# Decayed block attention ahead of two expert layers: the attention's outputs in two PSUM banks, one for each head parity

## The chip, the cores and the metric

The kernel runs on one core of a Trainium2 chip. The metric is the device time of one execution in microseconds (us), the median of three. The engines are named as the profile names them: PE (TensorE, the matrix engine; its weight loads are listed as PEld), DVE (VectorE), ACT (ScalarE), POOL (GpSimd) and SP (SyncE, which issues most of the DMAs).

## The reference

Three stages follow each other, all in fp32. The first is attention with a decay for each of 8 heads (batch 2, 768 positions, head size 64), worked out block by block with a state that is carried on:

```python
for b in range(nb):
    intra = einsum('bhic,bhjc->bhij', qb, kb) * Dmask
    intra = einsum('bhij,bhjd->bhid', intra, vb)
    inter = einsum('bhid,bhde->bhie', qb * lam_pow, kv_state)
    out[:, :, sl] = intra + inter
    kv_state = lam_block * kv_state + einsum('bhsd,bhse->bhde', kb * rev_pow, vb)
```

Its output, 1536 tokens of 512 values, goes through a dense mixture of 4 experts (every token through every expert, 512 to 1024 to 512, weighted by given probabilities), and then through a second mixture of 8 experts in which each token goes to the one that its gate chooses.

## The kernel before

**Stages.** The attention works in 12 chunks, named c, of 128 positions of one batch; even and odd c are the two batches. Its steps are mixed into the first unit of the first expert layer (k = 0, groups of 256 tokens at t0 = 0, 256 and 512). The list `asteps` and the table `paces` fix which attention step stands after which matmul group. The whole program is inside `tc.manual_schedule()`: each engine runs its instructions in the order in which the code lists them, so an instruction that waits holds up everything behind it on its engine. After the attention come the units of the first layer (PE lines 462 and 586), the routing, and the second layer.

**One chunk.** The 8 heads are held as 4 pairs h with a member r (0 or 1): head = 2h + r. Queries and keys of member r stand in partitions 64r to 64r+63.

- `att_qk(c)` (line 357): 8 products of keys by queries into two PSUM tiles, one for each r. Each uses 64 rows of the array and all 128 columns.
- `att_a(c)` (line 392): DVE multiplies these by the decay mask, into `a`.
- `att_qd(c)` and `att_kd(c)` (lines 368, 375): POOL makes the decayed queries `qd` and keys `kd`.
- `att_o(c)`: for c of 2 and more, 8 products of queries by state (line 410), each of 64 rows by 64 columns of the array with 128 columns streamed; then 8 products of values by `a` (line 416), each of 128 rows by 64 columns, added on top in PSUM. The output of a head is 64 partitions by 128 columns of the tile `xo`, one PSUM bank; member r has partitions 64r and up. So at line 410 a head with r = 0 uses the upper left quarter of the array and a head with r = 1 the lower right one. The result is then moved out of PSUM. For the first 6 chunks that is `hi_lo`: ACT rounds it into `xh` (line 171) and DVE takes the rest into `xl` (line 172). For the last 6 it is one ACT copy into `x2` (line 422).
- `att_u(c)`, for c below 10: 8 products of `kd` by values (line 434), 128 rows by 64 columns, 64 columns streamed, into the PSUM tile `u`, which has a bank of its own; DVE adds them to the decayed state (line 447, or copies them for c below 2, line 440), and POOL decays the state before (line 443).

At the very end of the second layer the last output tile `zr`, one PSUM bank, is moved out by two engines: DVE scales columns 0 to 255 (line 1265) and ACT columns 256 to 511 (line 1269), into separate halves of the result.

PSUM has 8 banks: 3 for `ps_mm`, 3 for `ps_qk`, and one each for `xo` and `u`. The tile framework puts a semaphore wait wherever two engines touch the same tile and it sees a conflict.

Each fp32 product is two matmul instructions on PE, each with its weight load, so the 8 products of a line are 16 instructions in the trace.

Of the kernel before, what the change touches and what calls it, by code (L numbers as in the profile page):

```python
# [8 lines left out]
F32 = mybir.dt.float32  # L9
# [9 lines left out]
P = 128  # L19
B, H, S, D = 2, 8, 768, 64  # L20
CH = 128
NCH = S // CH
NC = B * NCH
HP = H // 2
N = B * S
DM = H * D
KD = DM // P
E1, FF = 4, 1024
# [36 lines left out]
def body(ctx: ExitStack, tc: tile.TileContext, lam, att, dp, w1a, w2a, wg, wgt, w1b, w2b, out):  # L65
    nc = tc.nc
    V, A, G, T, SP = nc.vector, nc.scalar, nc.gpsimd, nc.tensor, nc.sync

    def pool(name, bufs, **kw):
        return tc.tile_pool(name=name, bufs=bufs, **kw)  # L70
# [6 lines left out]
    ps_mm = ctx.enter_context(pool("ps_mm", 3, space=PSUM))  # L77
# [83 lines left out]
    st = {}  # L161
# [8 lines left out]
    def hi_lo(hi, lo, src, eng):  # L170
        A.copy(out=hi, in_=src)  # L171
        eng.tensor_tensor(out=lo, in0=src, in1=hi.bitcast(F32), op=ALU.subtract)  # L172
# [122 lines left out]
    xh = xp.tile([P, KD, TS], F32R, name="xh")  # L295
    xl = xp.tile([P, KD, TS], F32R, name="xl")
    x2 = xp.tile([P, KD, TS], F32, name="x2")
# [4 lines left out]
    ps_qk = at_ctx.enter_context(pool("ps_qk", 3, space=PSUM))  # L302
    ps_xo = at_ctx.enter_context(pool("ps_xo", 1, space=PSUM))
# [8 lines left out]
    def load_att(c, half):  # L312
        if c >= NC:
            return
        t = ab.tile([P, 2, 512], F32, tag=f"att{half}", name=f"att{half}_{c}")
        at_t[c, half] = t
        SP.dma_start(out=t, in_=att[c, :, 2 * half:2 * half + 2, :])
# [26 lines left out]
    aw = {}  # L344
# [50 lines left out]
    def att_o(c):  # L395
        t = at_t[c, 1]
        v = t[:, 1, :].rearrange("p (h r d) -> p h r d", h=HP, r=2)
        first = c < B
        a = aw.pop((c, "a"))
        pl, tag = (ps_mm, "mm") if c == 1 else (ps_xo, "xo")  # L400
        xo = pl.tile([P, HP, CH], F32, tag=tag, name=f"xo{c}")


        heads = [(h, r) for h in range(HP) for r in range(2)]
        if not first:
            qd = aw.pop((c, "qd"))
            st = st_t[c]
            for h, r in heads:
                q = slice(64 * r, 64 * r + 64)
                T.matmul(  # L410
                    xo[q, h, :], st[q, h, :], qd[q, h, :], start=h == 0, stop=False,
                    skip_group_check=True,
                )
        for h, r in heads:
            q = slice(64 * r, 64 * r + 64)
            T.matmul(  # L416
                xo[q, h, :], v[:, h, r, :], a[r][:, h, :], start=first, stop=True,
                skip_group_check=not first,
            )
        g, o = divmod(c * CH, TS)  # L420
        if g:
            A.copy(out=x2[:, :, o:o + CH], in_=xo)
        else:
            hi_lo(xh[:, :, o:o + CH], xl[:, :, o:o + CH], xo, V)

    def att_u(c):
        t = at_t.pop((c, 1))
        v = t[:, 1, :].rearrange("p (h r d) -> p h r d", h=HP, r=2)
        if c < NC - B:
            kd = aw.pop((c, "kd"))  # L430
            u = ps_xo.tile([P, HP, D], F32, tag="u", name=f"u{c}")
            for h in range(HP):
                for r in range(2):
                    T.matmul(
                        u[64 * r:64 * r + 64, h, :], kd[:, h, r, :], v[:, h, r, :],
                        start=True, stop=True,
                    )
            sn = ab.tile([P, HP, D], F32, tag="st", name=f"st{c}", bufs=3)
            if c < B:
                V.tensor_copy(out=sn, in_=u)  # L440
            else:
                sd = st_t.pop(c)
                G.tensor_tensor(
                    out=sd, in0=sd,
                    in1=rq[:, :, CH - 1:CH].to_broadcast([P, HP, D]), op=ALU.mult,
                )
                V.tensor_tensor(out=sn, in0=sd, in1=u, op=ALU.add)
            st_t[c + B] = sn
        load_att(c + 2, 1)
# [431 lines left out]
    with tc.manual_schedule():  # L881
# [15 lines left out]
            out=upper, in_=upper, compare_op=ALU.is_ge, fill=1.0, base=0,  # L897
# [20 lines left out]
        att_a(0)  # L918
        att_a(1)
        att_o(0)  # L920
        att_kd(0)
        load_piece()
        load_piece()
        att_qd(0)
        att_o(1)
        split_to(0, 0)
        att_qd(1)
# [285 lines left out]
        def moe2_mm1_rows(e, h, hook):  # L1213
            hi, lo, _ = xg[e]
            wh, wl = wt[0, K1 + 2 * e + h]
            n = CAPS[e]
            ps = ps_mm.tile([P, 512], F32, tag="mm", name=f"gr{e}_{h}")
            for d in range(KD):
                mm3(ps[:n], [((hi[:, d, :], lo[:, d, :]), (wh[:, d, :], wl[:, d, :]))],
                    d == 0, d == KD - 1)  # L1220
                if d < KD - 1:
                    hook(h * KD + d)
            g = gp.tile([P, HF], F32, tag="gr", name=f"gr{e}_{h}")
            A.activation(out=g[:n], in_=ps[:n], func=AF.Relu)
            hook(h * KD + KD - 1)
            return g
# [83 lines left out]
        for e in range(E2):  # L1310
# [28 lines left out]
            if CAPS[e] <= P:  # L1339
                for h in range(2):  # L1340
                    g = moe2_mm1_rows(e, h, hook1)
# [22 lines left out]
    with tc.If(n_r > 0):  # L1364
        with pool("op", 1) as op:
# [12 lines left out]
                out=upto, in0=tiles_e, scalar1=float(P), scalar2=None, op0=ALU.mult  # L1378
            )
            V.tensor_copy(out=base, in_=upto)  # L1380
            for e in range(1, E2):
                V.tensor_tensor(
                    out=upto[:, e:e + 1], in0=upto[:, e:e + 1], in1=upto[:, e - 1:e], op=ALU.add
# [4 lines left out]
                out=pick, in0=desc.unsqueeze(1).to_broadcast([P, NC, E2]),  # L1388
# [3 lines left out]
                out=own_t, in0=pick, in1=base.unsqueeze(1).to_broadcast([P, NC, E2]), op=ALU.mult  # L1392
# [4 lines left out]
                out=own_t, in0=pick,  # L1397
# [5 lines left out]
                out=pos_o, in0=few, scalar=float(FAR), in1=slot, op0=ALU.mult, op1=ALU.add  # L1403
            )
            V.tensor_tensor(
                out=own, in0=steps.unsqueeze(2).to_broadcast([P, OMAX, E2]),
# [7 lines left out]
                out=rest.rearrange("(n p) w -> p n w", p=P),  # L1414
                in_=none.unsqueeze(1).to_broadcast([P, OMAX, W]),
            )
            for t in range(NC):
                G.indirect_dma_start(
                    out=rest, out_offset=bass.IndirectOffsetOnAxis(ap=pos_o[:, t:t + 1], axis=0),
                    in_=acc[:, t, :], in_offset=None, bounds_check=OMAX * P - 1, oob_is_err=False,  # L1420
                )
            with tc.For_i(0, n_r, 1) as i:
# [8 lines left out]
                for w, src in enumerate((w1b, w2b)):  # L1431
                    for h in range(2):
                        SP.dma_start(
                            out=ws[w][h],
                            in_=src[bass.ds(e_r, 1), h].rearrange("e p f m -> p (e f) m"),
# [16 lines left out]
                for f in range(2 * FC):  # L1452
                    T.matmul(
                        ps, ht[:, f, :], ws[1][f // FC][:, f % FC, :], start=f == 0,
                        stop=f == 2 * FC - 1,
# [3 lines left out]
                    out=y, in0=ps, scalar1=xb[:, DM:DM + 1], scalar2=None, op0=ALU.mult  # L1459
                )  # L1460
                G.indirect_dma_start(
                    out=out,
                    out_offset=bass.IndirectOffsetOnAxis(ap=xb.bitcast(I32)[:, DM + 1:W], axis=0),
                    in_=y, in_offset=None, bounds_check=N - 1, oob_is_err=False,
# [3 lines left out]
def layouts(q, k, v, lam, moe_domain_probs, moe_w1, moe_w2, moe2_w_gate, moe2_w1, moe2_w2):  # L1468
    import numpy as np

    def tposed(a):
        a = a.reshape(B, HP, 2, NCH, CH, D)
        return a.transpose(3, 0, 2, 5, 1, 4).reshape(NC, P, HP * CH)

    def plain(a):
        a = a.reshape(B, H, NCH, CH, D)
        return a.transpose(2, 0, 3, 1, 4).reshape(NC, CH, DM)

    def back(a):
        return a.reshape(B, H, NCH, CH, D)[:, :, :, ::-1].reshape(B, H, S, D)  # L1480

    kr, vr = back(k), back(v)
    att = np.stack([tposed(q), tposed(kr), plain(kr), plain(vr)], axis=2)

    def first(w):
        return w.reshape(-1, KD, P, 2, HF).transpose(0, 3, 2, 1, 4)

    def second(w):
        return w.reshape(-1, 2, FC, P, DM).transpose(0, 1, 3, 2, 4)

    return {
        "lam": np.concatenate(
            [np.tile(lam.reshape(HP, 2).T.reshape(1, H), (P, 1)),
             np.repeat(lam.reshape(HP, 2).T, D, axis=0)], axis=1),
        "att": att,
        "dp": moe_domain_probs.reshape(B, NCH, P, E1).transpose(2, 1, 0, 3).reshape(P, NC, E1),
        "w1a": first(moe_w1),
        "w2a": second(moe_w2),
        "wg": moe2_w_gate.reshape(KD, P, E2).transpose(1, 0, 2),
        "wgt": moe2_w_gate.T,  # L1500
        "w1b": first(moe2_w1),
        "w2b": second(moe2_w2),
    }
# [18 lines left out]
```

## Time and profile before

| | us |
|---|---|
| median of 3 runs (761.99 to 762.12) | 762.01 |
| the profiled execution, its own time | 761.43 |
| its span, first to last instruction | 759.6 |
| PE busy | 744.5 |
| DVE busy | 491.6 |
| ACT busy | 307.6 |
| POOL busy | 92.6 |

The span is the time between the first and the last instruction; the execution's own time lies 1.8 us above it. An engine's busy time counts neither its waits nor its register and semaphore instructions.

### The profile page before, as it was taken

To read this page: it belongs to the slowest core of one execution; us is meant where nothing else is said; L and a number is where in the kernel's file an instruction comes from. 1 tells how busy PE (TensorE), PEld (TensorE's weight loads), DVE (VectorE), ACT (ScalarE), POOL (GpSimd) and SP (SyncE) were. 2 spreads that over 40 slices of the span, in tenths; PEclk is the share of its full clock that TensorE was granted. 3 is DMA by queue.
4 is the path that set the end of the run, shared out by engine and by line. 5 is a ranking of instruction groups with operands and counts; after the bars stand their busy time and mean duration, and the time that the engine had idled before them with its cause. 6 is when DMAs were issued, how large, how long until landed. Compare 5 with 4: busy or idle time off the path is not lost.

```text
span 759.6 us, 12447 instructions
## 1 busy us (share of the span) xinstructions
PE 744.5 (98%) x4736; PEld 671.7 (88%) x4736; DVE 491.6 (65%) x1073; ACT 307.6 (40%) x664; POOL 92.6 (12%) x98
## 2 busy tenths in 40 slices
PE   8999999999999999999999999999999999999995
PEld 7888889898898988889898898988998998998994
DVE  6443277766757668565377777768457877675883
ACT  3222335353442535245132141522124756665673
POOL 4554320000000000000000000002111013121013
PEclk9999999999999999999999999999999999999998
DMA  9765107436361113016261633287113867855660
GB/s 299 258 223 167 57 35 269 166 140 249 111 249 57 56 55 106 34 50 233 120 242 62 236 103 148 75 282 241 43 55 117 296 220 227 309 184 185 241 223 29
DMA packets 34313, 122.59 MB, mean 161 GB/s; under 512 B 4113, under 2 KB 6161, under 8 KB 31179
## 3 DMA queue, kind: packets, MB, share of 16 engines
q1 hardware_dynamic: 32139, 115.47, 44.0%
q0 software_dynamic: 2112, 6.31, 2.2%
q8 instruction: 38, 0.62, 0.3%
q14 instruction: 24, 0.20, 0.1%
HBM read 96.04 MB, written 25.92 MB: 161 GB/s over the span
## 4 chain that ended last, share of the span: by engine, by line
PE 87%; issue 4%; DVE 4%; DMA 2%; SPq 1%; ACT 1%; POOL 0%; POOLq 0%; ACTq 0%
PE y L462 35%; PE b L586 21%; PE h L462 9%; PE g L462 5%; PE z L462 3%; PE zr L1255 2%; PE qk L357 1%; PE z L1179 1%; PE xo L416 1%; PE xo L410 1%; DMA att<-in_att 1%; PE g L1179 1%; DVE w1l L172 1%; PE gr L462 1%; PE xt L1161 1%
## 5 line engine op out<-in xcount | busy, mean ns | idle before, releaser
L503 DVE SCALAR_TENSOR_TENSOR acc<-y,p_sb,acc 128x512 f32<-128x512 f32 x84 | 63.0, 750 | 65.4 <-PE y L462 62.2
L172 DVE TENSOR_TENSOR w1l<-raw,w1h 128x512 fp32r<-128x512 f32 x124 | 82.6, 689 | 16.8 <-ACT w1h L171 16.5
L171 ACT CAST w1h<-raw 128x512 fp32r<-128x512 f32 x128 | 75.4, 617 | 0.0
L593 ACT COPY u<-b 128x384 f32<-128x384 f32 x66 | 31.1, 474 | 100.3 <-PE b L586 98.9
L462 PE MATMUL h<-xh,w0h 128*128 128x256 f32 (+1 forms) x208 | 57.9, 308 | 1.2 <-ACT w0h L171 1.2
L462 PE MATMUL h<-xh,w0l 128*128 128x256 f32 (+1 forms) x208 | 56.2, 299 | 0.0
L172 DVE TENSOR_TENSOR w0l<-raw,w0h 128x512 fp32r<-128x512 f32 x80 | 51.6, 684 | 6.6 <-ACT w0h L171 6.0
L171 ACT CAST w0h<-raw 128x512 fp32r<-128x512 f32 x98 | 55.7, 619 | 0.2
L586 PE MATMUL b<-xh,w0h 128*128 128x384 f32 x176 | 48.9, 338 | 0.0
L641 POOL IOTA places<- 128x7 f32 x1 | 0.2, 160 | 385.9 <-PE y L462 385.9
L112 POOL DMA_INDIRECT out<-y,xb x16 | 29.3, 1832 | 135.8 <-DVE y L1295 84.9
L462 PEld LDWEIGHTS h<-xh,w0h 128*128 128x128 f32 x208 | 38.2, 188 | 2.8 <-ACT w0h L171 1.4
L462 PEld LDWEIGHTS h<-xh,w0l 128*128 128x128 f32 x208 | 38.4, 189 | 0.4
L462 PE MATMUL g<-xg,w0h 128*128 128x288 f32 (+1 forms) x192 | 38.1, 293 | 0.0
L600 DVE TENSOR_TENSOR u<-b,u 128x384 f32<-128x384 f32 x66 | 36.4, 551 | 2.4 <-PE b L586 2.4
L462 PE MATMUL h<-xl,w0h 128*128 128x256 f32 (+1 forms) x208 | 37.0, 299 | 0.0
L677 DVE CUSTOM_DVE_ANT_0 x<-acc,x 128x512 f32<-128x512 f32 x48 | 32.9, 685 | 0.6
L586 PEld LDWEIGHTS b<-xh,w0h 128*128 128x128 f32 x176 | 32.3, 188 | 0.5
L462 PEld LDWEIGHTS h<-xl,w0h 128*128 128x128 f32 x208 | 31.2, 188 | 0.0
L462 PEld LDWEIGHTS g<-xg,w0h 128*128 128x128 f32 x192 | 30.8, 189 | 0.0
L586 PE MATMUL b<-xl,w0h 128*128 128x384 f32 x88 | 29.9, 339 | 0.0
L1179 PE MATMUL z<-g,w1h 128*128 128x352 f32 (+2 forms) x96 | 29.1, 366 | 0.7 <-DVE g L1201 0.6
(305 smaller groups left out, 2021.0 us busy)
## 6 DMA issues: line engine op xcount, KB each, us to landing
raw<-in_w2a SPq DMA_DIRECT2D x32, 512.0 KB, 3.5
raw<-in_w1b SPq DMA_DIRECT2D x32, 512.0 KB, 5.5
raw<-in_w2b SPq DMA_DIRECT2D x32, 512.0 KB, 5.0
att<-in_att SPq DMA_DIRECT2D x24, 512.0 KB, 5.0
raw<-in_w1a SPq DMA_DIRECT2D x22, 512.0 KB, 4.3
kept<-w0h SPq DMA_DIRECT2D x8, 1024.0 KB, 4.3
w0h<-kept SPq DMA_DIRECT2D x8, 1024.0 KB, 6.8
bins<-fill SPq DMA_DIRECT2D x1, 4626.0 KB
```

The costliest lines, as they stand in the source:

```text
L112: i = G.indirect_dma_start(out=dst, out_offset=bass.IndirectOffsetOnAxis(ap=idx, axis=0), in_=src, in_offset=None, bounds_check=rows - 1, ...
L171: A.copy(out=hi, in_=src)
L172: eng.tensor_tensor(out=lo, in0=src, in1=hi.bitcast(F32), op=ALU.subtract)
L357: T.matmul(qk[r][:, h, :], kT[64 * r:64 * r + 64, h, :], qT[64 * r:64 * r + 64, h, :], start=True, stop=True,)
L462: T.matmul(ps, l, r, start=first and i == 0, stop=last and i == len(ops) - 1)
L503: V.scalar_tensor_tensor(out=acc[:, t, 0:DM], in0=ps, scalar=p_sb[:, t, e:e + 1], in1=acc[:, t, 0:DM], op0=ALU.mult, op1=ALU.add,)
L586: T.matmul(ps, l[:, d, c], r[:, d, :], start=first and i == 0, stop=i == len(ops) - 1, skip_group_check=not first,)
L593: A.copy(out=t, in_=bank[2, s])
L600: V.tensor_tensor(out=t, in0=bank[b, s], in1=t, op=ALU.add)
L677: V.tensor_tensor_reduce(out=x2.rearrange("p d t -> p (d t)")[:, RING * DM:], in0=acc[:, t, 0:DM], in1=logit_piece(e), scale=1.0, scalar=0 ...
L1179: T.matmul(ps[:, :2 * n], wh, both, start=i == 0, stop=False)
L1255: T.matmul(ps[s][:st], l[:, c], r, start=h == 0 and j == 0, stop=h == 1 and j == len(ops) - 1)
```

## The change

- The output of a chunk goes into two tiles, `xo[0]` and `xo[1]`, each in a bank of its own, one for each r. Inside a tile a head pair h has partitions 64·(h mod 2) and up, and column block h div 2. So only 256 of the 512 columns of a bank are outputs.
- Line 410: of the four products with h = 0 and 1, r = 0 and 1, each lies on another quarter of the array, and so do those of h = 2 and 3.
- Line 416: the order is r outside, h inside.
- The move out of PSUM becomes two moves of half the size, one for each r.
- The tile `u` goes: for c of 2 and more its products are written into columns 256 to 511 of the bank of `xo[1]`; for c = 0 and 1 into a fresh tile in one of the two banks. For c = 1, `xo` takes two buffers of `ps_qk` in place of one of `ps_mm`.
- The order of the attention's output features changes with this, and the rows of the first layer's weights are reordered to match on the way in. Shapes and sizes of all DMAs stay.

```diff
-        pl, tag = (ps_mm, "mm") if c == 1 else (ps_xo, "xo")
-        xo = pl.tile([P, HP, CH], F32, tag=tag, name=f"xo{c}")
-        heads = [(h, r) for h in range(HP) for r in range(2)]
+        if c == 1:
+            xo = [ps_qk.tile([P, 512], F32, tag="qk", name=f"xo{c}_{r}") for r in range(2)]
+        else:
+            xo = [ps_xo.tile([P, 512], F32, tag=f"xo{r}", name=f"xo{c}_{r}") for r in range(2)]
+        if c >= B:
+            aw[c, "u"] = xo[1][:, 2 * CH:]
+        xo = [t[:, :2 * CH].rearrange("p (s i) -> p s i", s=2) for t in xo]
         if not first:
             qd = aw.pop((c, "qd"))
             st = st_t[c]
-            for h, r in heads:
-                q = slice(64 * r, 64 * r + 64)
+            for h in range(HP):
+                o = slice(64 * (h % 2), 64 * (h % 2) + 64)
+                for r in range(2):
+                    q = slice(64 * r, 64 * r + 64)
+                    T.matmul(
+                        xo[r][o, h // 2, :], st[q, h, :], qd[q, h, :], start=h < 2, stop=False,
+                        skip_group_check=True,
+                    )
+        for r in range(2):
+            for h in range(HP):
+                o = slice(64 * (h % 2), 64 * (h % 2) + 64)
                 T.matmul(
-                    xo[q, h, :], st[q, h, :], qd[q, h, :], start=h == 0, stop=False,
-                    skip_group_check=True,
+                    xo[r][o, h // 2, :], v[:, h, r, :], a[r][:, h, :], start=first, stop=True,
+                    skip_group_check=not first,
                 )
...
-        if g:
-            A.copy(out=x2[:, :, o:o + CH], in_=xo)
-        else:
-            hi_lo(xh[:, :, o:o + CH], xl[:, :, o:o + CH], xo, V)
+        for r in range(2):
+            d = slice(2 * r, 2 * r + 2)
+            if g:
+                A.copy(out=x2[:, d, o:o + CH], in_=xo[r])
+            else:
+                hi_lo(xh[:, d, o:o + CH], xl[:, d, o:o + CH], xo[r], V)
...
-            u = ps_xo.tile([P, HP, D], F32, tag="u", name=f"u{c}")
+            if c < B:
+                u = ps_xo.tile([P, 512], F32, tag=f"xo{1 - c}", name=f"u{c}")[:, 2 * CH:]
+            else:
+                u = aw.pop((c, "u"))
+            u = u.rearrange("p (h d) -> p h d", h=HP)
...
-        "w1a": first(moe_w1),
+        "w1a": first(
+            moe_w1.reshape(E1, 2, 2, 2, D, FF).transpose(0, 3, 1, 2, 4, 5).reshape(E1, DM, FF)
+        ),
```

## Rows read from the trace of the kernel before

**Rows 1.** The page: busy time, share of the span and instructions of each engine.

```profile
PE 744.5 (98%) x4736; PEld 671.7 (88%) x4736; DVE 491.6 (65%) x1073; ACT 307.6 (40%) x664; POOL 92.6 (12%) x98
```

**Rows 2.** Busy time in stretches of 4 us: engines, granted clock, DMA share, GB/s.

```profile
8.00:12.00 4.00, 2.59 (x40) 1.98 (x36) 2.50 (x5) 1.32 (x3) 1.06 (x1) 1.00 1.10 331
...
20.00:24.00 4.00, 4.00 (x63) 3.62 (x63) 1.40 (x4) 1.02 (x3) 3.08 (x4) 1.00 0.99 330
```

**Rows 3.** The chain that ended last, 0 to 90 us: start, length, what.

```profile
10.59 7.85 DMA att<-in_att
...
18.48 1.16 PE qk L357 x16
...
21.27 1.02 PE xo L410 x16
22.29 1.02 PE xo L416 x16
23.32 0.47 PE u L434 x16
...
81.89 1.02 PE xo L416 x16
```

**Rows 4.** The longest waits of PE in the whole span, by releaser.

```profile
PE y L462 <- ACT w1h L171: 1.4, 1, 1.4
PE h L462 <- ACT w0h L171: 1.2, 1, 1.2
```

**Rows 5.** Line 410 in stretches of 0.109 us: PE, PEld (x: running then), clock.

```profile
21.53:21.64 0.11, 0.11 (x7) 0.11 (x4) 1.00 1.29 451
...
21.85:21.96 0.11, 0.11 (x7) 0.11 (x4) 1.00 1.16 451
```

**Rows 6.** Order of time, PE, from 21.20 to 21.25 us.

```profile
21.20 0.33 PE L410 MATMUL xo<-qd,st 64*64 64x128 f32 x2
```

**Rows 7.** Groups by line and shape, 15 to 90 us: busy, mean ns, idle before.

```profile
L416 PE MATMUL xo<-a,att 128*64 128x128 f32 x160 | 10.9, 279 | 0.0
L410 PE MATMUL xo<-qd,st 64*64 64x128 f32 x160 | 10.9, 275 | 0.0
...
L434 PE MATMUL u<-att,kd 128*64 128x64 f32 x160 | 6.4, 223 | 0.0
...
L422 ACT COPY x<-xo 128x512 f32<-128x512 f32 x6 | 3.5, 586 | 9.2 <-PE xo L416 9.2
L447 DVE TENSOR_TENSOR st<-st,u 128x256 f32<-128x256 f32 x8 | 3.3, 415 | 9.4 <-PE u L434 5.1 <-POOL st L443 4.3
...
L172 DVE TENSOR_TENSOR xl<-xo,xh 128x512 fp32r<-128x512 f32 x4 | 2.8, 690 | 8.4 <-ACT xh L171 8.4
...
L469 ACT ACTIVATE ht_1h<-h 128x256 fp32r<-128x256 f32 x3 | 1.1, 383 | 5.7 <-PE h L462 5.7
```

**Rows 8.** Order of time, 20 to 29 us: chunk 2 from line 410 on.

```profile
21.20 1.09 PE L410 MATMUL xo<-qd,st 64*64 64x128 f32 x16
...
22.22 1.09 PE L416 MATMUL xo<-a,att 128*64 128x128 f32 x16
...
23.15 0.63 PE L434 MATMUL u<-att,kd 128*64 128x64 f32 x16
23.36 0.59 ACT L171 CAST xh<-xo 128x512 fp32r<-128x512 f32 x1 [1.67 <-PE xo L416]
...
23.98 0.69 DVE L172 TENSOR_TENSOR xl<-xo,xh 128x512 fp32r<-128x512 f32 x1 [1.84 <-ACT xh L171]
```

**Rows 9.** Order of time, 747 to 752.5 us: the last output tile `zr`.

```profile
751.25 0.49 DVE L1265 TENSOR_SCALAR y<-zr,xb 128x256 f32<-128x256 f32 x1 [2.89 <-PE zr L1255]
751.77 0.47 ACT L1269 ACTIVATE y<-zr,xb 128x256 f32<-128x256 f32 x1 [4.14 <-DVE y L1265]
```

**Rows 10.** Order of time, 11.2 to 12.5 us: PE held until ACT's first cast.

```profile
11.74 1.14 ACT L171 CAST w0h<-raw 128x512 fp32r<-128x512 f32 x2
...
12.42 0.39 PE L462 MATMUL h<-xh,w0h 128*128 128x256 f32 x1 [1.19 <-ACT w0h L171]
```

More of the change, by code (lines that the diff above doesn't have):

```diff
@@ L407, in att_o @@
             st = st_t[c]
-            for h, r in heads:
-                q = slice(64 * r, 64 * r + 64)
+            for h in range(HP):
[9 more added lines that the diff above has]
+                o = slice(64 * (h % 2), 64 * (h % 2) + 64)
                 T.matmul(
-                    xo[q, h, :], st[q, h, :], qd[q, h, :], start=h == 0, stop=False,
-                    skip_group_check=True,
-                )
[L414 to L419, printed above, removed]
-        g, o = divmod(c * CH, TS)
-        if g:
-            A.copy(out=x2[:, :, o:o + CH], in_=xo)
-        else:
-            hi_lo(xh[:, :, o:o + CH], xl[:, :, o:o + CH], xo, V)
+                    xo[r][o, h // 2, :], v[:, h, r, :], a[r][:, h, :], start=first, stop=True,
+                    skip_group_check=not first,
+                )
+        g, o = divmod(c * CH, TS)
+        for r in range(2):
[4 more added lines that the diff above has]
+                hi_lo(xh[:, d, o:o + CH], xl[:, d, o:o + CH], xo[r], V)
     def att_u(c):
```

## The prediction

> **What bounds the kernel now.** I read the page first: PE is busy for 744.5 of 759.6 us and the next engine, DVE, for 491.6 [rows 1]. Then the stretches of 4 us, to see whether that holds where the change is made: from 20 us on PE is busy for all 4.00 of 4.00 us at full granted clock (1.00, the 2.4 GHz level), while ACT, DVE and POOL have a quarter or more of the stretch free; before that PE still waits (2.59 of 4.00 from 8 to 12 us) [rows 2]. The chain of work says where one becomes the other: a load of queries and keys lands at 18.44 us (10.59 + 7.85), and from 18.48 us the chain is PE alone, group after group, past the last line 416 at 81.89 us [rows 3]. So in chunks 2 to 11 each microsecond that PE saves or waits moves all that follows. Whether it is lost again later is read from PE's waits: the longest in the span is 1.4 us, and the next, 1.2 us, lies before 18.48 [rows 4]. Chunks 0 and 1 have no work at line 410, and what they gain or lose lies before the load that lands at 18.44, so I count them at nothing; a loss there that outgrew that wait would cost its excess.
>
> **Line 410, the gain.** Today 16 matmul instructions run in 1.09 us from first start to last end, and the chain counts 1.02 us for them [rows 3, 8]. Two start together at 21.20 [rows 6]. In the later stretches of 0.109 us the counts stay the same from one to the next, 7 matmuls and 4 loads touched [rows 5], so two begin and two end in each: the two quarters of the array in use each take one instruction in 0.109 us. That makes 8 steps. On four quarters it would be 4 steps, and each chunk saves 4 x 0.109 = 0.44 us; over 10 chunks (160 instructions in [rows 7]) 4.4 us. The drain before line 416, which changes from quarters to halves of the array, stays.
>
> No row shows four quarters at once. What it needs is shown in parts: line 416 keeps the pace of 1.02 us with all 128 rows feeding two column halves, so the array takes as much input as four quarters want; and line 434, with 64 columns streamed, puts 16 loads and 16 matmuls into 0.47 us of the chain [rows 3], so loads and issue allow about 0.029 us an instruction, where four quarters ask for 0.109/4 = 0.027. The bounds are therefore 0 (the quarters that share rows or columns take turns) and 4.4 us (all four free); being nearest to line 434, I take 4.4 less a rounding, 4.3 us.
>
> The Trainium skill speaks against this, in "TensorE: Matmul & The Clock Gate", Part 3 (Packing small matmuls): a weight load overlaps matmuls in flight only when its row group differs. By that, the products of h = 0 and h = 1 with the same r would not run together and line 410 would save nothing: a sum of 769.3 us where mine is 764.9. The trace of before does not agree for halves: all products of line 416 use all 128 rows, and they run as fast as those of line 410, which differ in rows. I keep it as the second rival.
>
> **Line 416** keeps its 16 instructions on two column halves, 1.02 us. Only the order changes: `xo[0]` is complete 4 steps, 0.44 us, before `xo[1]`.
>
> **The two moves out of PSUM.** Each move of 128x512 becomes two of 128x256. No row has exactly these, so bounds. ACT: half of 0.586 is 0.29; the cast with relu at this size takes 0.383, the scaled copy of `zr` 0.47 [rows 7, 9]; I take 0.37, near the row of the same size and kind. DVE: half of 0.690 is 0.345, the same-size row, line 447, is 0.415 [rows 7]; I take 0.415. ACT then does some 0.15 us more for each of 12 chunks and DVE 0.14 us more for each of 6; both have free time there [rows 2], so this by itself costs nothing. If it stood on PE's path it would be 12 x 0.15 + 6 x 0.14, under 3 us.
>
> **The state products, the loss.** Today the products of line 434 go into their own bank and start at 23.15 us, 0.16 us before the end of line 416 at 23.31 (22.22 + 1.09), while ACT only begins to read `xo` at 23.36 and DVE reads it until 24.67 [rows 8]. After the change they are written into the bank that ACT and DVE still have to read, in other columns. Do other columns count as a conflict? The end of the trace answers: ACT's copy of columns 256 to 511 of `zr` was put down as waiting 4.14 us for DVE's read of columns 0 to 255 of the same bank, and started at 751.77, just after 751.25 + 0.49 = 751.74 [rows 9]. Nothing else links the two. So the waits go by bank, and line 434 must wait until the bank of `xo[1]` has been read. Behind it on PE, in order, stand `qk` of the next chunk and the first layer's matmuls: all of PE stops.
>
> How long, for chunks 2 to 5 (ACT, then DVE), with E the end of line 416: ACT starts at E + 0.05 (23.31 to 23.36 today), takes 0.37, DVE starts 0.03 later (23.36 + 0.59 = 23.95 to 23.98) and takes 0.415, PE follows after 0.06 (two overlapping casts take 1.14 from 11.74, so the first ends at 12.31 or a little later, and the matmul that waits for it starts at 12.42 [rows 10]: at most 0.11). That is E + 0.93, against E - 0.16 today: 1.09 us. Restarting costs some 0.05 more, as the first pair after a change of layout takes 0.33 where the mean is 0.275 [rows 6, 7]. Together 1.14 us. The move of `xo[0]` is out of the way by then: it starts 0.44 us earlier, so ACT is free at E and DVE at about E + 0.44, just when `xl` of `xo[1]` can start.
>
> For chunks 6 to 9 only ACT reads: E + 0.05 + 0.37 + 0.06 = E + 0.48, so 0.64 + 0.05 = 0.69 us. Chunks 10 and 11 have no such products, and in chunks 0 and 1 the fresh tile waits only for a move that ended long before.
>
> Sum: 4 x 1.14 + 4 x 0.69 = 7.3 us. With the shortest moves (0.29 and 0.345) it is 4 x 0.99 + 4 x 0.61 = 6.4; with ACT at 0.47, where `xo[0]` also begins to hold up `xo[1]`, 4 x 1.29 + 4 x 0.84 = 8.5.
>
> **Other waits.** `xo[1]` of the next chunk now also waits until DVE has read `u`; that is a `qk` group and a first-layer group earlier (over 2 us of PE work), so it costs nothing, and would cost up to a DVE group of 0.4 us a chunk if the two stood together. POOL's decay of the state starts after line 410 and so no later than today. DMAs are as many and as large; the two loads that a chunk sends for later follow PE by the same delay. The reordered weights are laid out before the launch. PE standing still for about 1 us should not cost clock: between 8 and 12 us it was idle for 1.41 us with the granted clock at 1.00 [rows 2].
>
> **Total:** -4.3 + 7.3 = +3.0 us. Against the profiled execution's 761.43 us (its span is 759.6) that is 764.4. The median of the runs shown is 762.01, 0.58 above that execution; the same +2.9 to 3.0 on it gives 764.9, my forecast. Its own range joins the bounds of the stall with those of the gain: +2.0 (6.4 less 4.4) to +5.2 (8.5 less 3.3, if the pairs follow each other so that 5 steps are needed), so 764.0 to 767.2.
>
> **The rivals.**
>
> 1. *Faster, 757.7 us.* Line 434 is not held, because the framework tells columns of a bank apart for PE as writer: then only the gain of 4.3 us is left. It decides if PE's restart comes within 0.4 us of the end of line 416. Rows 9 speak against it, two engines that touch no common column and yet wait. Chance 0.07.
> 2. *The four quarters do not work together, 769.3 us.* No gain, the whole stall of 7.3 us. The weight-load rule above would bring it; the halves of lines 416 and 434 speak against it [rows 3, 7]. Chance 0.14.
> 3. *The stall is hidden, about 762 us.* ACT and DVE finish sooner than I count, because the first half is moved while line 416 still runs, and a part of PE's delay is taken back where PE waits today for ACT's `w1h` (1.4 us [rows 4]). Both together give up to 6.4 - 1.4 - 4.4 = +0.6. But that wait begins at work that itself follows PE. Chance 0.13.
>
> **Numbers.** My forecast has 0.66. A measurement here can tell about 0.2% (1.5 us) from no change. Slower by more than that: forecast and rival 2, 0.80. Within: rival 3, 0.13. Faster: rival 1, 0.07. The range for 8 in 10 goes from 762.6, which leaves out rival 1 and two thirds of rival 3, to 769.8, which takes in about three quarters of rival 2 (762.0 with 6.4 to 8.5 is 768.4 to 770.5): 0.07 + 0.09 + 0.04 is left out.
>
> **What would show it.** In the changed profile line 410 should take about 0.6 us in the chain instead of 1.02, with four starts together; a gap before each line 434 should be put down to DVE (`xl`) in chunks 2 to 5 and to ACT (`x2`'s copy, line 422 today) in chunks 6 to 9, about 1.1 and 0.6 us; line 416 should not change. A missing gap makes rival 1 true, an unchanged line 410 rival 2, and a shorter idle time later on PE rival 3. What I would have wrong most easily is the pace of four quarters and the length of the short moves.

## The result, and the profile after

The changed kernel takes 766.12 us (median of 6 runs, 765.84 to 768.51) against 762.01 us: 4.11 us more, a ratio of the two medians of 1.0054. The ratio estimated from all runs is 1.0059, with a 95% interval of 1.0046 to 1.0072. The forecast was 764.9 us, its own range 764.0 to 767.2.

The chain of work of the changed kernel, 0 to 95 us (start, length, what), where [rows 3] has the chain of before; line 410 is now 415, line 416 is 422, line 434 is 446, line 422 is 430:

```profile
68.31 0.60 PE xo L415 x16
68.91 1.05 PE xo L422 x16
69.95 0.02 issue
69.98 0.38 ACT x L430
70.36 0.14 issue
70.49 0.69 PE xo L446 x16
71.18 1.09 PE qk L357 x16
...
85.80 1.02 PE xo L422 x16
```

Two things are new in a chunk. The queries by state count 0.60 us where they counted 1.02. And between the values by `a` and the state products the chain leaves PE: it goes through ACT's copy of `xo[1]` and 0.14 us more before PE goes on. The last piece began at 81.89 in [rows 3] and begins at 85.80 now: 3.91 us of the 4.11 are there when the attention ends.

That the first line really uses four quarters is seen in the order of time, PE alone, from 21.22 to 21.27 us; in [rows 6] two instructions had started there:

```profile
21.23 0.34 PE L415 MATMUL xo<-qd,st 64*64 64x128 f32 x4
```

The groups by line and shape, 15 to 90 us (busy, mean ns, idle time before and who ended it), answer to [rows 7]:

```profile
L422 PE MATMUL xo<-a,att 128*64 128x128 f32 x160 | 10.9, 279 | 0.0
...
L415 PE MATMUL xo<-qd,st 64*64 64x128 f32 x160 | 6.7, 282 | 0.0
L446 PE MATMUL xo<-att,kd 128*64 128x64 f32 x128 | 5.5, 226 | 6.3 <-ACT x L430 2.3 <-DVE xl L172 2.0 <-POOL qd L368 2.0
...
L430 ACT COPY x<-xo 128x256 f32<-128x256 f32 x12 | 4.5, 372 | 4.5 <-PE xo L422 4.1
...
L172 DVE TENSOR_TENSOR xl<-xo,xh 128x256 fp32r<-128x256 f32 x8 | 3.4, 425 | 4.2 <-ACT xh L171 4.2
...
L171 ACT CAST xh<-xo 128x256 fp32r<-128x256 f32 x8 | 3.0, 372 | 3.2 <-PE xo L422 2.9
```

Line 415 is busy for 6.7 us where it was 10.9, at nearly the same mean length of one instruction (282 ns, 275 before): more of them run side by side. Line 422 is unchanged. Line 446 had no idle time before it and now has 6.3 us. The profile puts part of that down to POOL's `qd`, on which these products do not depend: in chunks 2 to 5 PE waits 1.02 us each time, whether the profile names DVE (chunks 2 and 3) or POOL (chunks 4 and 5), so POOL's work only happened to end just before. In chunks 6 to 9 it is 0.56 us each time. Where the cause lies is seen in two chunks in order of time, chunk 2, where ACT and DVE read, and chunk 6, where ACT alone does:

```profile
21.82 1.09 PE L422 MATMUL xo<-a,att 128*64 128x128 f32 x16
...
22.53 0.81 ACT L171 CAST xh<-xo 128x256 fp32r<-128x256 f32 x2 [0.81 <-PE xo L422]
22.93 0.86 DVE L172 TENSOR_TENSOR xl<-xo,xh 128x256 fp32r<-128x256 f32 x2 [0.76 <-ACT xh L171]
...
23.94 0.69 PE L446 MATMUL xo<-att,kd 128*64 128x64 f32 x16 [1.02 <-DVE xl L172]
```

```profile
51.84 1.09 PE L422 MATMUL xo<-a,att 128*64 128x128 f32 x16
...
52.54 0.81 ACT L430 COPY x<-xo 128x256 f32<-128x256 f32 x2 [0.81 <-PE xo L422]
...
53.49 0.69 PE L446 MATMUL xo<-att,kd 128*64 128x64 f32 x16 [0.56 <-ACT x L430]
```

DVE's second move ends at 22.93 + 0.86 = 23.79 and PE restarts at 23.94; ACT's second copy ends at 52.54 + 0.81 = 53.35 and PE restarts at 53.49. From the end of line 422 it is 23.94 - 22.91 = 1.03 us and 53.49 - 52.93 = 0.56 us, where line 434 began 0.16 us before that end in [rows 8]: 1.19 and 0.72 us lost in a chunk, and 0.06 more because the group itself takes 0.69 us instead of 0.63. (The expectations below count the same gaps from the last start of line 422, 0.27 us before its end: 1.29 and 0.84 us, where [rows 8] has about 0.10.)

The profiled execution is the slowest of the six, 768.51 us. Its further 2.6 us arise between 580 and 605 us, in the routing: PE was busy for 0.91 of the 1.00 us from 588 us on, at a granted clock of 1.00, then the clock fell, to 0.50 (the 1.2 GHz level) from 590 to 594 us, and from 596 us on it was 1.00 again. The execution of before has 1.00 throughout these stretches, and so has every experiment's profile; nothing below rests on it.

### The profile page after: what moved, and what is told of

It reads as the page before. It is cut to its first block, busy times and chain, and to the rows that moved or that the text cites. A ratio compares the mean times of both kernels' runs of the same rounds, so it can differ in the third digit from the quotient of the medians.

```text
span 766.6 us, 12474 instructions
## 1 busy us (share of the span) xinstructions
PE 745.0 (97%) x4736; PEld 671.2 (88%) x4736; DVE 495.0 (65%) x1079; ACT 309.8 (40%) x676; POOL 92.7 (12%) x98
## 4 chain that ended last, share of the span: by engine, by line
PE 70%; issue 17%; POOL 2%; DVE 2%; ACT 1%; DMA 1%; POOLq 0%; SPq 0%; ACTq 0%
PE y L474 34%; PE b L598 21%; PE h L474 9%; POOL out L112 2%; PE g L1191 1%; PE qk L357 1%; PE z L1191 1%; PE xo L422 1%; DMA xe<-bins 1%; PE lg L712 1%; PE px L825 0%; PE xo L415 0%; PE xo L446 0%; PE g L1192 0%; PE z L1192 0%
```

## The experiments

The theory: four quarters save 0.42 us in each of 10 chunks (4.2 us), and the wait for the shared bank costs 1.25 us in four chunks and 0.78 in four others (8.1 us). Rivals: the halved moves cost the time, the saving is given back elsewhere, the wait is for something other than the bank. None of these kernels leaves out or changes a part of the computation.

**The state products in a bank of their own.** One thing undone, the sharing:

```diff
-        if c >= B:
-            aw[c, "u"] = xo[1][:, 2 * CH:]
...
-            if c < B:
-                u = ps_xo.tile([P, 512], F32, tag=f"xo{1 - c}", name=f"u{c}")[:, 2 * CH:]
-            else:
-                u = aw.pop((c, "u"))
-            u = u.rearrange("p (h d) -> p h d", h=HP)
+            u = ps_qk.tile([P, HP, D], F32, tag="qk", name=f"u{c}")
```

> The changed kernel with one thing undone: the state products (line 434 before) get a bank of their own again, a third buffer of the queries-by-keys pool, which is free at that point. Theory (the four quarters save 0.42 us in each of 10 chunks, and the wait for the shared bank costs 8.1 us): the gaps before the state products shrink from 1.29 and 0.84 us to 0.10 and only the gain is left, 762.0 - 4.2 = 757.8 us. Rival one (the halved moves out of PSUM, or the order of line 416, cost the time): it stays near 766. Rival two (the time saved at line 410 is given back later by PE's waits): about 762.

Measured: 757.55 us (757.46 to 757.73), ratio to before 0.9940, interval 0.9926 to 0.9954. Its chain, one chunk:

```profile
21.32 0.60 PE xo L413 x16
21.92 1.02 PE xo L420 x16
22.94 0.46 PE u L440 x16
23.41 1.09 PE qk L357 x16
```

The four groups stand end to end on PE with no other engine between them, and the gain is whole. This version is faster than both kernels: 4.5 us below the one before, 8.6 us below the changed one.

**Two quarters, bank still shared.** The other thing undone:

```diff
             for h in range(HP):
-                o = slice(64 * (h % 2), 64 * (h % 2) + 64)
                 for r in range(2):
                     q = slice(64 * r, 64 * r + 64)
                     T.matmul(
-                        xo[r][o, h // 2, :], st[q, h, :], qd[q, h, :], start=h < 2, stop=False,
-                        skip_group_check=True,
+                        xo[h // 2][q, h % 2, :], st[q, h, :], qd[q, h, :], start=h % 2 == 0,
+                        stop=False, skip_group_check=True,
                     )
-        for r in range(2):
-            for h in range(HP):
+        for h in range(HP):
+            for r in range(2):
...
-                    xo[r][o, h // 2, :], v[:, h, r, :], a[r][:, h, :], start=first, stop=True,
+                    xo[h // 2][q, h % 2, :], v[:, h, r, :], a[r][:, h, :], start=first,
```

> The changed kernel with the other thing undone: two banks, halved moves and the state products in the second bank stay, but the heads lie as before on two quarters of the array, and the weights are in their old order. Theory: line 410 takes 0.82 us from first to last start again, the gaps of 1.29 and 0.84 us stay: 762.0 + 8.1 = 770.1 us. Rival one (the same loss, from the moves): also about 770, so this run tells only the gain. Rival two (line 410 does not set the pace): about 766, as the changed kernel.

Measured: 770.19 us (770.14 to 770.25), ratio 1.0106, interval 1.0090 to 1.0121. Its chain, one chunk:

```profile
53.25 1.02 PE xo L414 x16
54.27 1.05 PE xo L421 x16
55.32 0.02 issue
55.34 0.38 ACT x L429
55.72 0.14 issue
55.85 0.69 PE xo L445 x16
```

Line 414 is at 1.02 again and the detour through ACT stays: the loss without the gain.

**Two quarters, state products in their own bank.** Both edits above together; of the change only the two banks and the halved moves are left.

> Both undone: heads on two quarters, state products in a bank of their own; only the two banks and the halved moves out of PSUM are left of the change. Theory: the moves are hidden, so 762.0 us, within 0.3. Rival one (the moves cost the time): 766 to 770.

Measured: 761.96 us (761.72 to 762.39), ratio 0.9999, interval 0.9990 to 1.0008. The halved moves cost nothing that can be measured (the interval allows 0.1% either way, under 0.8 us); rival one is out. The four kernels make a square. Four quarters save 770.19 - 766.12 = 4.1 us with the bank shared and 761.96 - 757.55 = 4.4 us without; sharing costs 770.19 - 761.96 = 8.2 us on two quarters and 766.12 - 757.55 = 8.6 us on four. The two effects add up, so the saving was not given back: it was outweighed.

**The state products beside the first output.** `aw[c, "u"] = xo[0][:, 2 * CH:]` in place of `xo[1]`, and nothing else.

> The changed kernel with the state products in the unused half of the first output bank in place of the second. Theory (the wait is for that bank's reads and for nothing else): the first bank is read one move earlier, 0.43 us (DVE) in chunks 2 to 5 and 0.40 us (ACT) in chunks 6 to 9, so the gaps fall to about 0.86 and 0.43 us and the time by 3.3 us: 762.8 us. Rival (the wait is for all moves of the chunk, or for some other work of ACT and DVE): no change from 766.1.

Measured: 762.34 us (762.16 to 762.72), ratio 1.0004, interval 0.9995 to 1.0013. Chunk 2 in order of time, and in the last line the state products of chunk 3:

```profile
22.57 0.81 ACT L171 CAST xh<-xo 128x256 fp32r<-128x256 f32 x2 [0.81 <-PE xo L422]
22.98 0.86 DVE L172 TENSOR_TENSOR xl<-xo,xh 128x256 fp32r<-128x256 f32 x2 [0.76 <-ACT xh L171]
...
23.55 0.69 PE L446 MATMUL xo<-att,kd 128*64 128x64 f32 x16 [0.59 <-POOL w1l L172]
...
30.54 0.69 PE L446 MATMUL xo<-att,kd 128*64 128x64 f32 x16 [0.58 <-DVE xl L172]
```

DVE's two moves run from 22.98 to 23.84, so the first ends near 23.41, and PE restarts at 23.55 while the second still reads the other bank. POOL's `w1l`, which the profile names, is not something that these products read; in chunk 3, where it names DVE, the wait is the same, 0.58 us. The moves themselves are where they were. So PE waits for the reads of the bank that it writes into, and for no other: 3.8 us come back from naming another bank, where 3.3 were expected. The waits of 0.59 and, in chunks 6 to 9, 0.14 us in place of 1.02 and 0.56 account for 3.4 of them.

Two things these runs do not show. Each of these tiles fills a bank, so they cannot tell a wait that goes by tile from one that goes by bank. And the wait is a semaphore wait that stands in the program; what would happen on the chip without it was not tried.

**The rows in turn.** The version with the bank of its own, with the loop at line 410 turned round:

```diff
-            for h in range(HP):
-                o = slice(64 * (h % 2), 64 * (h % 2) + 64)
-                for r in range(2):
-                    q = slice(64 * r, 64 * r + 64)
+            for r in range(2):
+                q = slice(64 * r, 64 * r + 64)
+                for h in range(HP):
+                    o = slice(64 * (h % 2), 64 * (h % 2) + 64)
```

> The version with the state products in their own bank (757.55 us), with the loop order of line 410 turned round: first the four products of r = 0, which all use the same 64 rows, then the four of r = 1. Theory (the quarters are four independent lanes and PE looks far enough ahead): the 16 instructions still take 0.40 us from first to last start, 757.6 us. Rival one (a weight load overlaps running matmuls only where the rows differ): the lanes with the same rows take turns and the group takes 1.6 us or more: 757.6 + 10 x 1.2 = 769 or more. Rival two (PE looks only a few instructions ahead, so the second half starts when the first is through): two lanes at a time, 0.82 us as before the change: 757.6 + 4.2 = 761.8.

Measured: 757.98 us (757.62 to 758.30), ratio 0.9947, interval 0.9933 to 0.9960. PE from 21.27 to 21.32 us:

```profile
21.28 0.35 PE L413 MATMUL xo<-qd,st 64*64 64x128 f32 x4
```

Four instructions still run at once, though the first products of the second row half stand behind four products (eight instructions) of the first half in the code. Both rivals are out. In the profiled execution the last line 420 begins 0.15 us later than in the order of the change (77.82 us against 77.67), of which 0.03 was there before the first of these groups: 0.01 us a chunk; the 0.4 us between the medians is near what these runs scatter.

**The state products one step later.** The changed kernel with the bank shared, but on PE the products follow the next chunk's queries by keys:

```diff
                 att_qk(c, (ps_qk, ps_qk))
+                if c > B:
+                    att_u(c - 1)
                 att_qd(c)
...
                 att_o(c)
-                att_u(c)
                 done["c"] = c
                 if c == NC - 1:
+                    att_u(c)
```

> The changed kernel, with the state products still in the second output bank, but issued one step later on PE, behind the queries by keys of the next chunk; nothing else moves except what follows these products (the state's update and the loads for the chunk after next). Theory (the whole loss is PE standing at the head of its queue until that bank is read): by then the bank is long read, the gaps are gone, and only the gain is left, 757.8 us. Rival (sharing the bank costs PE time in itself, or the later state and loads hold up the next chunk): between 759 and 766.

Measured: 759.12 us (758.61 to 759.70), ratio 0.9962, interval 0.9949 to 0.9976: faster than before, but 1.3 us more than the theory said. The chain, one chunk:

```profile
42.01 0.60 PE xo L415 x16
42.60 1.02 PE xo L422 x16
43.63 1.09 PE qk L357 x16
44.72 0.62 PE xo L446 x16
45.34 1.62 PE h L474 x12
```

No other engine stands in the chain, so the wait is gone, as the theory has it; but the time lies within the rival's range, by its lower end, and the rival's first part, that sharing costs PE time in itself, needs an answer. Line 446 now counts 0.62 us where line 440, the same products, counted 0.46 right behind line 420 in the chain of the first experiment: some 0.15 us more in each of 8 chunks, 1.2 us, which is the difference. It is the same 16 instructions. Behind the values by `a` they found the array in the layout that they use themselves (128*64 in the rows of both); behind the queries by keys (64*128) they do not. The first experiment has the same price where no bank is shared: in chunks 0 and 1 its line 440 stands behind the first layer's matmuls (128*128), and its chain has

```profile
15.74 0.62 PE u L440 x16
...
17.98 0.61 PE u L440 x16
```

So the price does not come from the shared bank. That the change of layout is what costs the 0.15 us fits these counts; it was not tried by itself.

## Why the prediction was right

**The gain** was taken at 4.3 us. Line 410 went from 1.02 to 0.60 us in the chain, 0.42 us times 10, and the square gives 4.1 to 4.4. The step that was read from the trace, four quarters at the pace of two, held. The rule of the Trainium skill in "TensorE: Matmul & The Clock Gate", Part 3, that a weight load overlaps running matmuls only when its row group differs, is what the second rival went by, with nothing of the gain left; no run here agrees with it: quarters with the same rows start together, in the order of the change (x4 at 21.23) and with the rows in turn (x4 at 21.28).

**The loss** was taken at 7.3 us and came out as 4 x (1.19 + 0.06) + 4 x (0.72 + 0.06) = 8.1. The mechanism was the one forecast, PE held at the head of its queue by the reads of the bank, shown by the first and the fourth experiment. The moves were sized well: ACT 0.372 us (0.37 taken), DVE 0.425 (0.415 taken), and that they do not cost anything by themselves was shown by the third. The reason given for that was read too kindly from [rows 2]: from 20 to 24 us POOL is busy for 3.08 of 4.00 us, and from 24 to 28 us DVE for 3.62, so less than a quarter is free there. The term that was too small is "PE follows after 0.06": it is 0.14 to 0.15 us, 0.08 more in each of 8 chunks, about 0.65 of the missing 0.8 us. The row that I had taken it from was a PE wait for one engine alone; another wait, put down to DVE alone, is shorter still in the chain of before (DVE's `ht_3l` ends at 113.17 + 0.48 = 113.65 us, PE goes on at 113.69). Here the products depend on two, POOL's `kd` and the reader of the bank, and PE's queue has an instruction more, which line 440 of the first experiment has not:

```profile
L446 PEldq EVENT_SEMAPHORE  x8: 51/51/51, 23.8 to 76.0; - x8
```

Eight, one for each chunk with the wait, of 51 ns. That these, or the second engine at all, are the reason for the 0.08 us was not tried.

**What was counted at nothing** was nothing: line 422 kept its pace, chunks 0 and 1 did not move the start (the first `qk` behind the load begins at 18.50 us, 18.48 in [rows 3]), and `xo[1]` of the next chunk never waited for the state's sum.

**The rivals.** The first, that columns of a bank are told apart, fell with the gaps in the trace. The reading of `zr` in [rows 9] came out right, but it was less sure than it said: DVE and ACT there also write two halves of one output tile, `y`, so something else did link the two. In the changed kernel PE and the readers meet in the PSUM tile alone, and PE waits. The second fell with the four starts. The third asked for shorter gaps and for PE's later waits to take some of the delay back; the gaps were longer, and the delay of 3.91 us at the end of the attention was still 4.1 us in the median. Forecast 764.9, measured 766.12: of the 1.2 us of difference 0.8 is the stall and 0.1 the gain; the rest lies within the scatter of the runs.

## What to carry to other kernels

Packing small products on more quarters of the array paid here by the step count, and the step is read from stretches of the trace; but the PSUM that it takes must come from a buffer that is free at that time, not from unused columns of a bank that other engines are about to read. Here a wait at the head of PE's queue cost what was left of the readers' work, their hand-overs and the restart, 0.78 to 1.25 us a chunk, so find out who still reads the bank before putting a matmul into it. Where there is no bank left, look for a rotating pool in which a buffer lies idle in that step; in these runs that took 757.55 us, moving the products behind other work 759.12, sharing the bank that is read first 762.34, and sharing the one that is read last 766.12.

## What was not expected of the hardware

- Four quarters keep the step of two: 4 instructions in 0.109 us, the line 0.60 us instead of 1.02 in the chain, also when the order of the code puts all products of one row half first (0.68 us from first start to last end against 0.67).
- The place of a group among others has a price: 16 short instructions count 0.46 us behind a group of the same layout and 0.61 to 0.62 behind two others.
- PE took 0.14 to 0.15 us to go on after each wait for the bank, against at most 0.11 in [rows 10] and 0.04 at 113.65 us of the kernel before, where one engine is named; the reason was not tried.
